# Gating a spatial MLP: the gate value is evicted to one bf16 tile before it is multiplied with z1

## The chip, the core and the metric

The kernel runs on one core of a Trainium2 chip. The metric is device time in microseconds (us), the median of three executions. Engines are named as in the profile: PE is TensorE (matmuls; PEld are its weight loads), DVE is VectorE, ACT is ScalarE, POOL is GpSimd, SP is the engine that issues most of the DMAs.

## The reference

The block first adds a memory-augmented attention to its input and then a gated MLP. The change concerns the MLP alone, whose computation is this (2048 tokens, D = 1024, F = 3584, Fh = 1792):

```
z  = gelu(layernorm(h) @ w_in)                 # [2048, 3584]
z1 = z[:, :1792]
z2 = layernorm(z[:, 1792:])
g  = w_sp @ z2 + b_sp[:, None]                 # over tokens: [2048, 2048] @ [2048, 1792]
h2 = h + (z1 * g) @ w_out
```

Inputs and output are bf16. `z1 * g` is the product that the change is about.

## The kernel before

**The order of the work.** The program is written by hand as a sequence of calls on five engines. A recorder (`_Recorder`, from L30) notes each call with the tiles that it reads and writes, and works out which semaphores it must wait for: the last writer of what it reads, and the last writer and all readers of what it overwrites (`record`, L87; `dep`, L112). For readers and writers on the same engine it waits as well, TensorE excepted; a wait that an earlier instruction of that engine already implies is dropped. `emit` then issues each engine's calls in the recorded order. Each engine thus has one fixed in-order queue, and all instructions show up in the profile under one line, L210, where the recorder issues them; groups are told apart by the names of the tiles.

**The stages.** Attention comes first (to about 340 us of the profile), then the z2 half of the MLP's first matmul with its layernorm, then the z1 half, which leaves z1 transposed in the tile `z1T` (F on the partitions, tokens along the free axis). The first gating stage (`gate(0)`, L1283) gates the first 1024 tokens and writes the product over `z1T` in bf16. Sixteen output units multiply that by `w_out`. The second gating stage (`gate(1)`, L1423) does the other 1024 tokens and writes f16 into `z1x`, which is the same memory under a 16-bit float type of another kind. A last stage multiplies it by `w_out` and writes the output.

**A gating stage.** The product `w_sp @ z2` is done as a two by two block product by seven multiplications in place of eight (Strassen's scheme in Winograd's form). The weight blocks b11, b12, b22, b21 and their sums t1 to t4 are f16 tiles; the sums of z2 blocks (`ss`) are made by VectorE. There are seven groups `g` of 128 columns of F per half. In each, seven products (`prod`, eight matmuls of 128x128 by 128x512 each) go to PSUM banks in the order t2, t1, p1 of a later group (b11), t3, p2 of the next group (b21), t4, b22. Groups 4 and 5 of the second stage have one product fewer. Four output blocks leave each group (c11 is that of the next group): half `i` of F by half `t` of the tokens. Each is made by

- `stt` (L1091): VectorE's scalar_tensor_tensor, one PSUM bank times the scale `inv`, plus a tile. It takes a bank's value down to SBUF and releases the bank, or the accumulation into it, to TensorE.
- `out` (L1094): VectorE's tensor_tensor, the value times a 128x512 part of `z1T`, into `z1T` or `z1x`.

Values and intermediate sums lie in 2 KB fp32 tiles: `u2`, `u3`, `s1b1`, `s1b2`, `s1` (`TMP`, L396; in the profile `tmp_u`, `tmp_s1b`, `tmp_s`). `s1` is p1 scaled, copied from PSUM by ScalarE (`copy1`). POOL adds the bias rows `brow` to it and gets `s1b1` and `s1b2`, which two of the values start from. One group on VectorE runs: `stt` into u2; sums for `ss`; further jobs handed in by the caller (`each`: in the second stage sums of w_out blocks, `ob_sum`, L1376, and in group 6 sums of gated blocks, `y_sum`, L1392); `stt` twice into u3 and `out`; a sum; `c11` of the next group; `stt` into s1b1 and `out`; `stt` into u2 and `out`. TensorE's t4 must wait until the first `stt` of t3 has read bank `bb`, and t3 until `stt` has read t2's value in the same bank.

POOL's add into `s1b1` for the next group overwrites the tile that `out` reads; its add into `s1b2` overwrites one that only `stt` reads.

**Behind the second stage** the last group's sums (`y_sum` on POOL, for one column block) and `o_adds` (L1444, POOL) come before the first output blocks.

Of the kernel before, what the change touches and what calls it, by code (L numbers as in the profile page):

```python
# [5 lines left out]
BF16 = mybir.dt.bfloat16  # L6
# [10 lines left out]
L = 512  # L17
# [241 lines left out]
def bass_sequential_preLN__memory_aug_infini_attn__mixer_gmlp__prompt_kernel(  # L259
# [19 lines left out]
    K = 1024  # L279
# [4 lines left out]
    def tens(name, shape, dt, off):  # L284
        sz = int(np.prod(shape[1:])) * mybir.dt.size(dt)
        assert off % 32 == 0 and off + sz <= ARENA, (name, off, sz)
        t = nc.alloc_sbuf_tensor_at(name, list(shape), dt, offset=abase + off)
        R.space[t[:].tensor.name] = ("sbuf", off)
        return t

    class Bump:
# [4 lines left out]
        def __call__(self, name, shape, dt):  # L296
# [73 lines left out]
          for k, o in ROLES + (("t1", 118), ("t2", 190), ("t3", 22), ("t4", 38))}  # L370
# [24 lines left out]
    BSQ = tens("bsq", [128, 2], F32, 896)  # L395
    TMP = {k: tens("tmp_" + k, [128, L], F32, (4 + 2 * i) * K)  # L396
           for i, k in enumerate(("s1", "s1b1", "s1b2", "u2", "u3"))}
    SJ = [tens("sj%d" % i, [128, T], BF16, (4 + 4 * i) * K) for i in range(2)]
    BROW = [tens("brow%d" % i, [128, L], BF16, (205 + i) * K) for i in range(2)]
    WO0 = [tens("w_out0%d" % i, [128, 7, 512], BF16, o * K) for i, o in enumerate((54, 198))]  # L400
# [10 lines left out]
    def bank(b):  # L411
        return PS[:, b, :]
# [7 lines left out]
    def next_bank():  # L420
        b = rot["banks"][rot["n"] % len(rot["banks"])]
        rot["n"] += 1
        return b
# [333 lines left out]
    vb = [next_bank() for _ in range(2)]  # L757
# [175 lines left out]
    def sp_norm_load(r):  # L933
        sp.dma_start(SJ[r % 2][:], B_w_sp[r * 128:(r + 1) * 128, :])

    def sp_norm(r):
        act.activation(SJ[r % 2][:], SJ[r % 2][:], ACTF.Square, accum_out=SQ[:, r:r + 1])

# [128 lines left out]
    def a_blk(i, j, g):  # L1067
        f = 896 * i + 128 * g
        return Z2H[:, 8 * j:8 * j + 8, f:f + 128]

    def s_sum(k, g):
        if k == 1:
            dve.tensor_tensor(SS[:, 0], a_blk(1, 0, g), a_blk(1, 1, g), ALU.add)
        elif k == 2:
            dve.tensor_tensor(SS[:, 1], SS[:, 0], a_blk(0, 0, g), ALU.subtract)
        elif k == 3:
            dve.tensor_tensor(SS[:, 2], a_blk(0, 0, g), a_blk(1, 0, g), ALU.subtract)
        else:
            dve.tensor_tensor(SS[:, 3], a_blk(0, 1, g), SS[:, 1], ALU.subtract)

    def prod(b, a, w, first):
        for i in range(8):
            pe.matmul(bank(b), a[:, i, :], BH[w][:, i, :], start=(first and i == 0), stop=(i == 7),
                      skip_group_check=True)

    def gate(pr, seam=lambda: None, mid=lambda: None, each=lambda g, k: None):
        inv, zo = (INV[0], Z1T) if pr == 0 else (INVY, Z1X)
        t1, t2 = slice(1024 * pr, 1024 * pr + 512), slice(1024 * pr + 512, 1024 * pr + 1024)
        s1, s1b1, s1b2, u2, u3 = (TMP[k][:] for k in ("s1", "s1b1", "s1b2", "u2", "u3"))

        def stt(o, b, add):  # L1091
            dve.scalar_tensor_tensor(o, bank(b), inv[:], add, ALU.mult, ALU.add)

        def out(v, g, i, t):  # L1094
            dve.tensor_tensor(zo[:, g + 7 * i, t], v, Z1T[:, g + 7 * i, t], ALU.mult)

        def ss(k, g):
            if g < 7:
                s_sum(k, g)

        def p1(g):
            prod(g % 3, a_blk(0, 0, g), "b11", True)

        def copy1(g):
            act.activation(s1, bank(g % 3), ACTF.Copy, scale=inv[:])

        def p2(g):
            prod(g % 3, a_blk(0, 1, g), "b21", False)

        def c11(g):  # L1110
            stt(u3, g % 3, BROW[0][:])
            out(u3, g, 0, t1)

        p1(0)
        copy1(0)
        pool.tensor_tensor(s1b2, s1, BROW[1][:], ALU.add)
        pool.tensor_tensor(s1b1, s1, BROW[0][:], ALU.add)
        p1(1)
        if not pr:
            p1(2)  # L1120
        seam()
        p2(0)
        c11(0)
        for g in range(7):
            bb, bc = 3 + g % 2, 5 + g % 2
            prod(bb, SS[:, 1], "t2", True)
            prod(bc, SS[:, 0], "t1", True)
            stt(u2, bb, s1b2)
            if g == 0:
                mid()  # L1130
            ss(4, g)
            if g:
                ss(1, g + 1)
                ss(2, g + 1)
            if 1 - pr <= g <= 3:
                p1(g + 2)
            each(g, 0)
            prod(bb, SS[:, 2], "t3", False)
            if g < 5:
                copy1(g + 1)  # L1140
                p2(g + 1)
            elif g == 5:
                p1(6)
                copy1(6)
            else:
                p2(6)
            each(g, 1)
            stt(u3, bb, s1b2)
            stt(u3, bc, u3)
            out(u3, g, 1, t2)  # L1150
            if not g:
                ss(1, 1)
                ss(2, 1)
            if g < 6:
                pool.tensor_tensor(s1b2, s1, BROW[1][:], ALU.add)
            ss(3, g + 1)
            if g != 5:
                c11(min(g + 1, 6))
            prod(bb, a_blk(1, 1, g), "t4", False)
            each(g, 2)  # L1160
            stt(s1b1, bb, s1b1)
            out(s1b1, g, 1, t1)
            if g < 6:
                pool.tensor_tensor(s1b1, s1, BROW[0][:], ALU.add)
            prod(bc, SS[:, 3], "b22", False)
            stt(u2, bc, u2)
            out(u2, g, 0, t2)
            each(g, 3)

    fins = {}  # L1170
# [97 lines left out]
    def seam():  # L1268
        sp_half("b21")
        for k in range(1, 4):  # L1270
            s_sum(k, 0)

    def mid():
        for r in range(4):
            sp_sum("t4", r)

    def z1_norm(g, k):
        for h in range(k and 2):
            r, o = 2 * g + (k > 2), 1024 + 512 * h
            if k != 2:  # L1280
                act.activation(bank(7), Z1T[:, r, o:o + 512], ACTF.Square, accum_out=SQY[:, 2 * r + h:2 * r + h + 1])

    gate(0, seam, mid, z1_norm)  # L1283
    pool.tensor_copy(TW[:], TOT[:])
    fin_load(units[0], act)
# [135 lines left out]

    sp.dma_start(Z1T[:, :, 0:512], wout[:, :, 512:D])
    gate(1, each=each1)  # L1423

    def o_prod(b, a, w, first, lo=0, hi=512, cs=range(7)):
# [42 lines left out]
    for g in range(4):  # L1468
        bb, bc = 3 + g % 2, 5 + g % 2
# [63 lines left out]
```

## Time and profile before

| | |
|---|---|
| median of three executions | 758.6 us (758.08 to 759.28) |
| profiled execution | 757.02 us, span 755.3 us |
| TensorE busy | 748.4 us (99%), granted clock 9 of 9 tenths in every slice |
| VectorE busy | 573.4 us (76%) |
| ScalarE, POOL busy | 421.4 us (56%), 294.0 us (39%) |
| first gating stage | about 489 to 574 us |
| second gating stage | about 624 to 710 us |
| in its group 2 (657 to 669 us) | VectorE 11.76 of 12.00 us busy, POOL 2.31, ScalarE 0.69 |

How to read it: a line of the groups gives engine, operation, output tile <- input tiles with partitions x elements and type, the count, then busy time and the mean ns of one, then the engine's idle time before them and what ended it. A timeline line is start, duration (or, for several in a row, their common stretch), engine, operation, tiles and count; in brackets the idle time before it and what ended it. The chain that ended last is followed back from the last instruction: at each step to what released it, or to the instruction before it on its engine. Its lines give start, length and owner. Buffer numbers are left out of tile names, so `tmp_u` is u2 or u3, and `tmp_s1b` is s1b1 or s1b2.

### The profile page before, as it was taken

The page shows a single profiled execution, that of the slowest core. Times are in us where ns is not written, and L with a number is a line of the kernel's source. Part 1 is how long each engine was busy: PE and PEld are TensorE (multiplying, and loading weights), DVE is VectorE, ACT ScalarE, POOL GpSimd, SP SyncE. Part 2 cuts the span into 40 slices and gives each one's busy share as a digit, 9 for nine tenths or more (in the row PEclk, how much of TensorE's full clock was granted, in tenths as well). Part 3 has the DMA queues.
Part 4 walks back from the last instruction along what each step waited for, and adds up shares of the span by engine and source line. Part 5 has one row for each costly group of instructions (what it writes and reads, how often), then busy time and mean ns, then how long its engine had stood idle before and what let it go on. Part 6 is the DMA issues. An engine that isn't in the chain of part 4 may idle for free.

```text
span 755.3 us, 13486 instructions
## 1 busy us (share of the span) xinstructions
PE 748.4 (99%) x5470; PEld 357.9 (47%) x5470; DVE 573.4 (76%) x1013; ACT 421.4 (56%) x519; POOL 294.0 (39%) x450
## 2 busy tenths in 40 slices
PE   8999999999999999999999999999999999999998
PEld 4445455555554445555554444444444444443444
DVE  5585589768974576768896796998895575999876
ACT  6777877787777767226994879723330525300000
POOL 2564456555654333010049988522120001122342
PEclk9999999999999999999999999999999999999999
DMA  9654556454424331678640026320029950001111
GB/s 304 173 160 91 85 78 139 94 79 92 113 58 96 115 72 43 178 195 254 195 141 0 1 56 126 68 86 1 0 41 171 234 196 15 0 1 55 64 49 56
DMA packets 136783, 75.09 MB, mean 99 GB/s; under 512 B 98064, under 2 KB 126480, under 8 KB 136720
## 3 DMA queue, kind: packets, MB, share of 16 engines
q1 hardware_dynamic: 129184, 67.14, 36.9%
q10 hardware_dynamic: 7536, 7.08, 3.2%
q8 instruction: 43, 0.70, 0.4%
q14 instruction: 20, 0.16, 0.1%
HBM read 42.74 MB, written 8.39 MB: 68 GB/s over the span
## 4 chain that ended last, share of the span: by engine, by line
PE 88%; DVE 10%; DMA 1%; issue 1%; POOL 0%; ACT 0%; ACTq 0%; DVEq 0%; POOLq 0%
PE ps L210 88%; DVE z1x L210 3%; DVE tmp_u L210 3%; DVE ss L210 2%; DMA wv<-in_A_wv_dram 1%; DVE tmp_s1b L210 1%; DVE z2h L210 0%; POOL ot L210 0%; DVE sy L210 0%; POOL sy L210 0%; ACT L210 0%; DVE ot L210 0%; DVE fin L210 0%; ACTq L210 0%; DVEq L220 0%
## 5 line engine op out<-in xcount | busy, mean ns | idle before, releaser
L210 ACT ACTIVATE e<-ps 128x2048 bf16<-128x2048 f32 (+1 forms) x96 | 152.7, 1590 | 41.7 <-PE ps L210 41.5
L210 POOL TENSOR_SCALAR_AFFINE_SELECT e<-e 128x512 bf16<-128x512 bf16 x128 | 90.6, 721 | 131.4 <-ACT e L210 131.4
L210 PE MATMUL ps<-win,hnT 128*128 128x448 bf16 x512 | 98.4, 353 | 0.0
L210 POOL TENSOR_TENSOR tmp_s1b<-tmp_s,brow 128x512 f32<-128x512 f32 x28 | 33.6, 1203 | 129.7 <-DVE tmp_u L210 57.4
L210 PEld LDWEIGHTS ps<-win,hnT 128*128 128x128 bf16 x512 | 49.6, 98 | 46.3 <-issue 0.2
L210 PE MATMUL ps<-xnT,wk 128*128 128x512 bf16 x256 | 60.8, 381 | 0.0
L210 PE MATMUL ps<-xnT,wq 128*128 128x512 bf16 x256 | 60.5, 379 | 0.0
L210 PE MATMUL ps<-wv,xnT 128*128 128x512 bf16 x256 | 59.8, 380 | 0.4 <-DVE xnT L210 0.3
L210 DVE TENSOR_TENSOR zt<-ps,zt 128x512 f32<-128x512 f32 x70 | 48.2, 689 | 15.7 <-PE ps L210 12.1
L210 PE MATMUL ps<-wo,oT 128*128 128x512 bf16 x256 | 58.0, 380 | 0.0
L210 ACT ACTIVATE z<-ps 128x448 bf16<-128x448 f32 x60 | 30.6, 548 | 35.0 <-PE ps L210 35.0
L210 PE MATMUL ps<-w_out,z1T 128*128 128x512 bf16 x224 | 48.6, 379 | 0.0
L210 DVE BATCH_NORM_STATS2 zst<-z 128x6 f32<-128x448 bf16 x64 | 38.0, 612 | 10.9 <-ACT z L210 10.9
L210 PEld LDWEIGHTS ps<-v,e 128*128 128x128 bf16 x1280 | 38.8, 96 | 14.0 <-issue 6.5
L210 DVE RECIPROCAL rd<-ps 128x16 f32<-128x16 f32 x32 | 8.0, 250 | 47.1 <-PE ps L210 46.9
L210 ACT ACTIVATE tmp_s<-ps,invy 128x512 f32<-128x512 f32 x7 | 4.8, 687 | 68.0 <-POOL tmp_s1b L210 37.8
L210 PE MATMUL ps<-v,e 128*128 128x33 bf16 x1280 | 42.2, 178 | 0.0
L210 POOL TENSOR_TENSOR sz<-wzh 128x512 f16<-128x512 f16 x28 | 34.5, 1231 | 8.4 <-PE ps L210 8.4
L210 PEld LDWEIGHTS ps<-wo,oT 128*128 128x128 bf16 x256 | 24.0, 98 | 27.6
L210 PEld LDWEIGHTS ps<-xnT,wk 128*128 128x128 bf16 x256 | 22.6, 98 | 29.9 <-issue 5.0
L210 ACT ACTIVATE z1T<-zt,inv 128x512 bf16<-128x512 f32 x42 | 29.0, 715 | 13.1 <-DVE zt L210 13.1
L210 PEld LDWEIGHTS ps<-wv,xnT 128*128 128x128 bf16 x256 | 23.1, 98 | 27.3 <-DVE xnT L210 0.8
(206 smaller groups left out, 1478.0 us busy)
## 6 DMA issues: line engine op xcount, KB each, us to landing
sj<-in_B_w_sp_dram SPq DMA_DIRECT2D x16, 512.0 KB, 3.6
xch<-in_A_x_dram SPq DMA_DIRECT2D x16, 256.0 KB, 3.4
xr<-in_A_x_dram SPq DMA_DIRECT2D x16, 256.0 KB, 3.9
out_dram<-hch SPq DMA_DIRECT2D x16, 256.0 KB, 2.6
win<-in_B_w_in_dram SPq DMA_DIRECT2D x4, 896.0 KB, 5.3
wz<-in_B_w_in_dram SPq DMA_DIRECT2D x6, 512.0 KB, 7.9
wo<-in_A_wo_dram SPq DMA_DIRECT2D x1, 2048.0 KB, 8.4
fin<-out_dram ACTq DMA_DIRECT2D x16, 128.0 KB, 3.0
```

The source lines that it names most:

```text
L210: ins = getattr(e, op.name)(*op.args, **op.kw)
```

## The change

A new tile `VB`, 128x512 in bf16 (1 KB per partition), lies at offset 61 KB, which no tile in use during the gating stages covers. The second `stt` of each output block, whose result is the gate value, writes into it in place of the fp32 tile; `out` reads it there. The first `stt` of u2 and u3, `s1` and POOL's adds stay in fp32. Both gating stages use the same single tile for all four values. `stt` and `out` are as before.

```diff
+    VB = tens("vb", [128, L], BF16, 61 * K)
...
         def c11(g):
-            stt(u3, g % 3, BROW[0][:])
-            out(u3, g, 0, t1)
+            stt(VB[:], g % 3, BROW[0][:])
+            out(VB[:], g, 0, t1)
...
             stt(u3, bb, s1b2)
-            stt(u3, bc, u3)
-            out(u3, g, 1, t2)
+            stt(VB[:], bc, u3)
+            out(VB[:], g, 1, t2)
...
             prod(bb, a_blk(1, 1, g), "t4", False)
             each(g, 2)
-            stt(s1b1, bb, s1b1)
-            out(s1b1, g, 1, t1)
+            stt(VB[:], bb, s1b1)
+            out(VB[:], g, 1, t1)
             if g < 6:
                 pool.tensor_tensor(s1b1, s1, BROW[0][:], ALU.add)
             prod(bc, SS[:, 3], "b22", False)
-            stt(u2, bc, u2)
-            out(u2, g, 0, t2)
+            stt(VB[:], bc, u2)
+            out(VB[:], g, 0, t2)
```

VectorE's instructions are the same in number and order. In the changed program's list the evictions for s1b1 and u2 gain a wait for VectorE's own preceding product, and the first eviction of u2 in the following group loses one.

## The prediction

> **What bounds the kernel now.** I read the page's busy line first, then the chain that ended last in order of time, then TensorE's timeline over both gating stages, then the groups by shape, then the whole timeline of one gating group.
>
> ```profile
> PE 748.4 (99%) x5470; PEld 357.9 (47%) x5470; DVE 573.4 (76%) x1013; ACT 421.4 (56%) x519; POOL 294.0 (39%) x450
> ```
>
> TensorE is never long idle, so no change on VectorE can win more than TensorE's gaps. Where they are, the chain says:
>
> ```profile
> 8.85 625.99 PE ps L210 x4892
> ...
> 634.87 0.76 DVE tmp_u L210
> ...
> 712.02 0.70 DVE z1x L210
> ...
> 716.12 36.09 PE ps L210 x175
> ```
>
> Up to 634.8 us and after 716 us the chain is TensorE alone. Between, which is the second gating stage, it runs through VectorE without a break, ending in POOL's short adds (712.8 to 715.2). There VectorE is late and TensorE is stopped now and then. Busy time hides this, as a matmul's modelled end reaches into the next one; starts show it. In TensorE's timeline eight matmuls normally start in 1.727 us (216 ns each):
>
> ```profile
> 689.54 1.89 PE L210 MATMUL ps<-t1h,ss 128*128 128x512 f16 x8
> 692.08 1.90 PE L210 MATMUL ps<-t3h,ss 128*128 128x512 f16 x8 [0.65 <-DVE tmp_u L210]
> ...
> 713.87 1.89 PE L210 MATMUL ps<-z1x,sy 128*128 128x512 f16 x8
> 716.12 1.69 PE L210 MATMUL ps<-z1x,sy 128*128 128x512 f16 x7 [0.36 <-DVE ot L210]
> ```
>
> 689.54 to 692.08 is 2.54 us, so 0.81 lost; 713.87 to 716.12 is 2.25, so 0.52 lost. All blocks of the two stages read this way give, in the second: before t4 of group 1, 0.64; t3 and t4 of group 4, 0.34 and 0.32; t3 and t4 of group 5, 0.81 and 0.06; t3 of group 6, 0.11; and 0.08 for the blocks behind the stops, which start 0.013 us apart more: 2.36 us. In the first stage t3 of groups 4 and 5 lose 0.10 each, with their tails 0.23. Behind the second, 0.52. Sum 3.11 us: the ceiling.
>
> [...] Both kinds are in the trace:
>
> ```profile
> L210 DVE TENSOR_TENSOR z1T<-tmp_u,z1T 128x512 bf16<-128x512 f32 x21 | 17.9, 852 | 0.7
> ...
> L210 DVE TENSOR_TENSOR z1x<-tmp_s1b,z1T 128x512 f16<-128x512 f32 x7 | 4.8, 692 | 0.2
> ...
> L210 DVE SCALAR_TENSOR_TENSOR fin<-ps,invo,fin 128x512 bf16<-128x512 f32 x4 | 3.0, 749 | 2.0 <-PE ps L210 2.0
> ...
> L210 DVE TENSOR_TENSOR z1x<-z1x 128x512 f16<-128x512 f16 x2 | 0.8, 418 | 0.0
> ```
>
> So a 16-bit product of 512 takes 418 ns against 692, and an eviction that writes bf16 takes 749, the same as the 748 of one that writes fp32: narrowing is free, the product gains. [...]
>
> ```profile
> 661.74 0.96 DVE L210 TENSOR_TENSOR z1x<-tmp_u,z1T 128x512 f16<-128x512 f32 x1
> 662.62 0.68 DVE L210 TENSOR_TENSOR ss<-z2h 128x1024 f16<-128x1024 f16 x1
> ...
> 664.00 0.69 DVE L210 TENSOR_TENSOR z1x<-tmp_u,z1T 128x512 f16<-128x512 f32 x1
> 664.61 0.75 DVE L210 SCALAR_TENSOR_TENSOR tmp_s1b<-ps,invy,tmp_s1b 128x512 f32<-128x512 f32 x1
> 665.38 0.69 DVE L210 TENSOR_TENSOR z1x<-tmp_s1b,z1T 128x512 f16<-128x512 f32 x1
> 666.00 0.74 DVE L210 SCALAR_TENSOR_TENSOR tmp_u<-ps,invy,tmp_u 128x512 f32<-128x512 f32 x1
> 666.15 1.16 POOL L210 TENSOR_TENSOR tmp_s1b<-tmp_s,brow 128x512 f32<-128x512 f32 x1 [4.01 <-DVE z1x L210]
> ...
> 666.77 1.09 DVE L210 TENSOR_TENSOR z1x<-tmp_u,z1T 128x512 f16<-128x512 f32 x1
> 667.89 0.75 DVE L210 SCALAR_TENSOR_TENSOR tmp_u<-ps,invy,tmp_s1b 128x512 f32<-128x512 f32 x1
> ```
>
> Products clear of POOL take 0.69; the one at 666.77, half under POOL's add, takes 1.09. Evictions, with one input in PSUM, are not slowed. [...] Without a wait the next one starts 0.61 us after a product of 0.69 (664.00 to 664.61), with one it starts 0.02 after its end (667.86 to 667.89): a wait costs 0.10. [...]
>
> **The change part by part.**
>
> *The product.* Per group four products hold VectorE, from their start to that of the next instruction, for 0.61 (c11), 0.62 (s1b1), 1.12 (u2), 0.88 (u3): 3.23 us. At 418 ns they are slots of 0.35 without a wait behind, 0.44 with one.
>
> *The waits.* One tile `vb` takes all four values, so each eviction into it must wait until the product before has read it. On VectorE's own order that is a wait on itself. In the changed program's instruction list the evictions for s1b1 and u2, right behind a product, newly carry it (0.44 slots); the first eviction of the next group loses the one it had (u2's slot goes to 0.35); u3's product is followed by a sum (0.35). Nothing but VectorE's own queue stands behind these waits. `vb` lies where the last z1 stage had an input of TensorE, which TensorE has long read when the first gating product it waits for anyway is done: nothing.
>
> *POOL's add into s1b1* waited for the product; now the eviction alone reads `tmp_s1b1`, so the add starts some 0.7 us sooner and lies over s1b1's product in place of u2's. It is not on the path (its sum is next read some 10 us later); its cost is the contention. Lower bound: none, a 0.44 slot. Upper: the trace has a 16-bit sum that takes 0.68 alone and 1.65 wholly under POOL, 41% of the rate; the fp32 product at 666.77 had 0.54 us under POOL and did 0.14 us of work there, 26%. At 41% the 0.42 product takes about 1.02, at 26 to 30% 1.2. I take 1.02, a slot of 1.04. u2's product is then free. POOL's other add starts with the eviction before u3's product and outlives it by 0.39; at the same rate u3's product takes 0.65, a slot of 0.58 (0.35 to 0.60).
>
> *Sum per group:* 0.44 + 1.04 + 0.35 + 0.58 = 2.41, so 0.82 saved (0.6 to 1.65). Over groups 1 to 3 of the second stage VectorE now needs 12.12, 11.86 and 11.86 us (starts of the first u2 eviction at 643.92, 656.04, 667.89, 679.75) where TensorE needs seven blocks, 12.09. In groups 4 and 5 there is one block fewer, 10.36, against VectorE's 11.52 and 10.56: hence the stops. With 0.82 less, VectorE catches up in groups 1 to 3, and group 4 asks for 10.70 against 10.36: 0.34 late, under the slack. That slack is one block, 1.73, less 0.17 for the last matmul's end, 0.77 for the eviction and about 0.08 to TensorE: 0.7. So the stops of both stages go, with perhaps 0.1 left in group 5: 2.36 + 0.23 - 0.1 = 2.5.
>
> *The tail.* In group 6 POOL adds nothing, so its products take 0.42; four of them behind the last t3 bring the last product's end forward by about 1.15 us, and with it POOL's three sums and its add, for which TensorE lost 0.52 at 716.12. What is late next is VectorE's eviction of the first output block: it needs TensorE's product that ends near 714.04, then 0.75 for it and 0.75 for the next one, and TensorE can go on at 715.68 in place of 715.60. So 0.44 is won.
>
> *Everything else* (DMAs, ScalarE, matmuls) issues the same instructions; what VectorE saves beyond this becomes its own idle time. Total 2.5 + 0.4 = 2.9 to 3.0. The profiled execution took 757.02 us with a span of 755.3, so 754.0 and 752.3 are expected; the median, 758.6, lies 1.6 above that execution and the same 3.0 comes off it: 755.6.
>
> **The rivals.** *Part of it.* The contention is at its upper end (1.2) and group 5 still stops TensorE, or the stops of t3 and t4 in groups 4 and 5 (1.6 us) halve only. For it: the 0.7 slack is nearly used there. Against: even the upper end saves 0.6 a group. 756.2 to 757.4.
>
> *The product stays at full length*: mixed types (bf16 by bf16 into f16 in the second stage), or writing over its own input in the first. Against: the profile has 16-bit sums from bf16 into f16 at 680 ns for 1024. Then VectorE has only the new waits, about 0.1 a group net: 758.2 to 759.2.
>
> *Slower: POOL locks s1b1's product out.* POOL's add, now side by side with the product, could hold it until it is done and be stretched as well, as when beside the 16-bit sums (two adds in 2.96 us, against 1.155 alone). The product's slot would be 1.6 + 0.44, u3's 0.8 + 0.44 - together 3.3, where 2.44 is the point at which VectorE needs more than now (3.23 - 0.44 - 0.35). It would lose 0.83 a group, 5.8 us over the seven groups of the second stage, where VectorE already sets the pace: about 764. Against: the 16-bit sum wholly under two adds got through in 1.65 while they ran.
>
> *More.* The median's extra 1.6 us over the profiled execution could lie in these same stops: down to 754.0.
>
> **How the numbers follow.** Forecast (755.0 to 756.3) 0.70; part 0.14; unchanged 0.07; slower 0.05; more 0.04. 0.2%, about what a measurement of this kernel can tell from no change, is 1.5 us. Faster: 0.70 + 0.11 + 0.04 = 0.85; same 0.03 + 0.07 = 0.10; slower 0.05. The range takes forecast and part, 0.84: 754.6 to 757.4.
>
> **What would show it.** Products near 0.42 us and s1b1's between 0.42 and 1.2; VectorE's busy time 12 to 24 us lower; POOL's s1b1 add right behind the eviction; no t3 or t4 block over 1.8 us after the one before; a chain that is TensorE nearly throughout. Products of 0.69, or gaps that stay while VectorE idles between, would refute it.

## The result, and the profile after

The changed kernel takes 755.35 us (755.01 to 755.98, four runs) against 758.94 for the kernel before (758.08 to 759.71, four runs): a ratio of 0.9954, 95% interval 0.9937 to 0.9971. A later measurement gave 755.65 (five runs) against 758.45 (seventeen), 0.9962 (0.9949 to 0.9974). The changed kernel is faster by about 3 us.

The profiled execution took 755.45 us with a span of 753.7, only 1.6 us shorter than before's 755.3. The other 1.4 us are not in the gating: in that execution the first gating stage began at 490.76 us, before's at 489.34. Over all profiles below, of kernels that are the same up to there, it began between 489.34 and 493.28. In after's profile TensorE waits 1.0 us, just before 412.06, for one of POOL's sums of the z1 stage; in before's the only trace of that wait is 0.4 us of a weight load. That is a part of it; the rest is not traced here. This scatter belongs to no version, so I compare traces over the stretch from the first gating product to the end of the span, called the tail stretch below. It is 265.9 us before (from 489.34 to 755.29) and 262.9 after (from 490.76 to 753.67); here and below it is taken from the traces before rounding. These are the two lines its starts come from, each out of TensorE's timeline, first before and then after:

```profile
489.34 4.91 PE L210 MATMUL ps<-b11h,z2h 128*128 128x512 f16 x22
```

```profile
490.76 3.62 PE L210 MATMUL ps<-b11h,z2h 128*128 128x512 f16 x16
```

The busy line of the page after, VectorE 16.3 us lower:

```profile
PE 748.3 (99%) x5470; PEld 359.1 (48%) x5470; DVE 557.1 (74%) x1013; ACT 421.6 (56%) x519; POOL 296.3 (39%) x450
```

The chain that ended last, after: from 412 us to the last output VectorE is no longer in it.

```profile
412.06 338.53 PE ps L210 x1578
750.62 0.62 DVE fin L210
```

TensorE's timeline after, at the places where before showed 2.54 and 2.25 us between starts. 689.47 to 691.20 is 1.73, one normal block; the fifteen matmuls from 712.78 take 3.24 us, 216 ns each. What is left of the stops is one of 0.09 us, at 684.28, 1.81 after the block before:

```profile
682.47 1.89 PE L210 MATMUL ps<-b21h,z2h 128*128 128x512 f16 x8
684.28 1.90 PE L210 MATMUL ps<-t4h,z2h 128*128 128x512 f16 x8
...
689.47 1.89 PE L210 MATMUL ps<-t1h,ss 128*128 128x512 f16 x8
691.20 1.89 PE L210 MATMUL ps<-t3h,ss 128*128 128x512 f16 x8
...
712.78 3.40 PE L210 MATMUL ps<-z1x,sy 128*128 128x512 f16 x15
716.02 1.67 PE L210 MATMUL ps<-w_out0h,z1x 128*128 128x512 f16 x7
```

The groups by shape, after. The products have a mean of 482 ns where most had 869; the evictions are as long as ever:

```profile
L210 DVE TENSOR_TENSOR z1x<-vb,z1T 128x512 f16<-128x512 bf16 x28 | 13.5, 482 | 1.0
...
L210 DVE SCALAR_TENSOR_TENSOR vb<-ps,invy,tmp_u 128x512 bf16<-128x512 f32 x14 | 10.5, 751 | 1.0 <-PE ps L210 0.5
```

And the same group as was shown of before, in the whole timeline:

```profile
661.05 1.16 POOL L210 TENSOR_TENSOR tmp_s1b<-tmp_s,brow 128x512 f32<-128x512 f32 x1 [6.59 <-DVE tmp_u L210]
...
661.79 0.70 DVE L210 TENSOR_TENSOR z1x<-vb,z1T 128x512 f16<-128x512 bf16 x1
...
663.79 0.42 DVE L210 TENSOR_TENSOR z1x<-vb,z1T 128x512 f16<-128x512 bf16 x1
664.25 0.75 DVE L210 SCALAR_TENSOR_TENSOR vb<-ps,invy,tmp_s1b 128x512 bf16<-128x512 f32 x1
665.03 0.42 DVE L210 TENSOR_TENSOR z1x<-vb,z1T 128x512 f16<-128x512 bf16 x1
665.08 1.40 POOL L210 TENSOR_TENSOR tmp_s1b<-tmp_s,brow 128x512 f32<-128x512 f32 x1 [2.87 <-DVE vb L210]
...
666.28 0.48 DVE L210 TENSOR_TENSOR z1x<-vb,z1T 128x512 f16<-128x512 bf16 x1
...
667.13 0.75 DVE L210 SCALAR_TENSOR_TENSOR tmp_u<-ps,invy,tmp_s1b 128x512 f32<-128x512 f32 x1 [0.37 <-PE ps L210]
```

The last line shows the roles reversed: VectorE now waits for TensorE (0.37 us) ahead of the eviction that in before it reached too late. The line at 665.03 is the surprise: this product lies under POOL's add and still takes 0.42; it is the add that takes 1.40.

### The profile page after: what moved, and what is told of

Its sections match the earlier page's. It is cut to its first block, busy times and chain, and to the rows that moved or that the text cites. A ratio compares the mean times of both kernels' runs of the same rounds, so it can differ in the third digit from the quotient of the medians.

```text
span 753.7 us, 13510 instructions
## 1 busy us (share of the span) xinstructions
PE 748.3 (99%) x5470; PEld 359.1 (48%) x5470; DVE 557.1 (74%) x1013; ACT 421.6 (56%) x519; POOL 296.3 (39%) x450
## 4 chain that ended last, share of the span: by engine, by line
PE 90%; DMA 3%; ACT 3%; DVE 2%; POOL 2%; issue 0%; ACTq 0%; DVEq 0%
PE ps L210 90%; DMA sj<-in_B_w_sp_dram 2%; ACT sj L210 2%; POOL zrs L210 1%; DMA wv<-in_A_wv_dram 1%; POOL sz L210 1%; DVE zst L210 1%; ACT z L210 1%; DVE wzh L210 1%; DVE ht L210 0%; DVE zmv L210 0%; ACT L210 0%; DVE fin L210 0%; ACTq L210 0%; DVE top L210 0%
## 5 line engine op out<-in xcount | busy, mean ns | idle before, releaser
L210 POOL TENSOR_TENSOR tmp_s1b<-tmp_s,brow 128x512 f32<-128x512 f32 x28 | 36.4, 1301 | 121.6 <-DVE tmp_u L210 63.0
```

Source lines behind the costliest of these rows:

```text
L210: ins = getattr(e, op.name)(*op.args, **op.kw)
```

## The experiments

My theory: TensorE's stops, nearly all in and behind the second stage, are the whole gain, and they go because VectorE spends less time per group. The rivals: VectorE time counts everywhere alike; the separate tile, not the short product, is what helps; a part of the gain is only the new place of POOL's add. The kernel before was timed beside each of them; ratios are to those runs.

### One stage alone

Two kernels that use `VB` in one stage and the fp32 tiles in the other:

```diff
+        def vb(o):
+            return VB[:] if pr == 1 else o      # or pr == 0
-            stt(VB[:], bc, u3)
-            out(VB[:], g, 1, t2)
+            stt(vb(u3), bc, u3)
+            out(vb(u3), g, 1, t2)
```

and so for the other three values.

> The bf16 value in the second gating stage alone, fp32 in the first. Theory (the gain is TensorE's stops, which lie nearly all in the second stage and behind it): 2.7 to 3.0 us under the kernel before, that is near 755.8, with the 0.10 us stops before t3 of groups 4 and 5 of the first stage still there. Rival (every microsecond that VectorE saves counts, in either stage alike): half of the gain, near 757.1.

> The bf16 value in the first gating stage alone. Theory: only the first stage's 0.2 us of stops go, so 0.0 to 0.4 us under the kernel before, near 758.5; the stops of the second stage stay at about 2.4 us and 0.5 behind it. Rival (saved VectorE time counts alike in both): half of the gain, near 757.1.

Measured: second stage alone 755.92 us against 758.30, ratio 0.9967 (0.9955 to 0.9980); first stage alone 758.16, ratio 0.9997 (0.9988 to 1.0005). Tail stretches: 263.1 and 265.7 us. So the second stage brings 2.8 us (2.4 by the medians) and the first 0.2 of the 3.0; saved VectorE time does not count alike. The stops stay where the theory puts them. TensorE's timeline of the kernel with the first stage alone, group 5 of the second stage:

```profile
691.19 1.89 PE L210 MATMUL ps<-t1h,ss 128*128 128x512 f16 x8
693.73 1.90 PE L210 MATMUL ps<-t3h,ss 128*128 128x512 f16 x8 [0.65 <-DVE tmp_u L210]
```

2.54 us again, to the hundredth. And of the kernel with the second stage alone, group 4 of the first stage, 1.83 us between the starts, 0.10 more than a block:

```profile
546.30 1.89 PE L210 MATMUL ps<-t1h,ss 128*128 128x512 f16 x8
548.13 1.90 PE L210 MATMUL ps<-t3h,ss 128*128 128x512 f16 x8
```

### The tile without the short product

```diff
-            dve.tensor_tensor(zo[:, g + 7 * i, t], v, Z1T[:, g + 7 * i, t], ALU.mult)
+            dve.scalar_tensor_tensor(zo[:, g + 7 * i, t], v, 1.0, Z1T[:, g + 7 * i, t], ALU.mult, ALU.mult)
```

> The changed kernel, tile, waits and types kept, but the product done by a scalar_tensor_tensor (value times 1.0 times z1), [...]690 to 760 ns in place of 420. Theory (the length of the product is what counts): the stops come back, 758.5 to 760. Rival (the separate tile counts, since it frees the fp32 tiles and lets POOL's add into s1b1 start before the product): stays at 755.4 to 756.0.

Measured: 757.23 us (21 runs), ratio 0.9986 (0.9980 to 0.9993); tail stretch 264.8. Products at full length:

```profile
L210 DVE SCALAR_TENSOR_TENSOR z1x<-vb,z1T 128x512 f16<-128x512 bf16 x28 | 21.0, 751 | 1.0
```

Neither forecast holds. My theory said that all stops come back, the rival that none does; 1.2 of the 3.0 us of gain are left. The stop before t3 of group 5 is 0.59 in place of 0.81, those of the first stage are gone. The timeline of this kernel's second stage explains a part: the product for u2 takes 0.74 and not 1.09, since POOL's add now falls on s1b1's product, which is not lengthened.

```profile
666.34 0.69 DVE L210 SCALAR_TENSOR_TENSOR z1x<-vb,z1T 128x512 f16<-128x512 bf16 x1
666.38 1.66 POOL L210 TENSOR_TENSOR tmp_s1b<-tmp_s,brow 128x512 f32<-128x512 f32 x1 [3.40 <-DVE vb L210]
```

### The short product without the tile

Each eviction writes bf16 into the front half of its own fp32 tile:

```diff
-    VB = tens("vb", [128, L], BF16, 61 * K)
+    VB = {k: tens("vb_" + k, [128, L], BF16, o * K) for k, o in (("s1b1", 6), ("u2", 10), ("u3", 12))}
```

with `stt` and `out` taking the tile of their value.

> bf16 values without the shared tile: each eviction writes bf16 into the front half of the fp32 tile that the kernel before used (u3, s1b1, u2), so the added waits of VectorE on itself go and POOL's add into s1b1 again waits for the product. Theory: products stay at 420 ns, TensorE is the bound, the time is that of the changed kernel, 755.2 to 755.8. Rival 1 (the single tile's waits, some 0.2 us a group, are on the path): about 1 us faster, 754.3. Rival 2 (POOL's earlier add is a part of the gain): 756.5 or more.

Measured: 755.41 us (seven runs), ratio 0.9967 (0.9955 to 0.9979); tail stretch 262.9, that of the changed kernel. Both rivals fall: the single tile's waits are hidden, and POOL's earlier add is not needed once the product is short. Here the add is back behind s1b1's product and u2's product pays for it, at 0.82 or 0.66 us as the case may be; the path does not notice:

```profile
656.15 1.16 POOL L210 TENSOR_TENSOR tmp_s1b<-tmp_s,brow 128x512 f32<-128x512 f32 x1 [3.21 <-DVE z1x L210]
656.77 0.82 DVE L210 TENSOR_TENSOR z1x<-vb_u,z1T 128x512 f16<-128x512 bf16 x1
```

### POOL's earlier add alone

To see what of the 1.2 us came from the order of POOL's add: the kernel before, all in fp32, with

```diff
-            stt(s1b1, bb, s1b1)
-            out(s1b1, g, 1, t1)
+            stt(u3, bb, s1b1)
+            out(u3, g, 1, t1)
```

> The kernel before, all in fp32, with one edit: the eviction for s1b1 writes u3 (free then) and its product reads it there, so that POOL's add into s1b1 starts beside that product, as in the changed kernel. If the full-length experiment's 1.1 us came from this order alone: s1b1's product 0.69 with POOL's add stretched to about 1.66, u2's product near 0.74 in place of 1.09, some 0.9 to 1.1 us under the kernel before (757.4), and from the first gating matmul to the end 264.8 to 265.0 us in place of 265.9. If most of it came from the wait that the next group's first eviction loses: less than half of that, 758.2, 265.4 or more.

Measured: 757.86 us (13 runs) against 758.45, ratio 0.9991 (0.9983 to 0.9999); tail stretch 265.1, so 0.8 us of the 1.2, a little less than expected. s1b1's product takes 0.69 with an add of 1.66 beside it, as expected; u2's takes 0.87, not 0.74. In the full-length experiment two more things differ: the next group's first eviction has no wait on u2's product, and its products are another operation. The traces point to the first for the remaining 0.3 to 0.4 us. From s1b1's product to the next group's first eviction it is 2.18 us there (654.70 to 656.88) and 2.30 here (654.33 to 656.63), and that eviction starts 0.07 us before the end of u2's product there and 0.04 after it here. A run that changes this wait alone was not made, so it is not shown.

### More and less VectorE time

Three kernels move VectorE's time per group and leave the product's type alone. The changed kernel with an unneeded eviction:

```diff
             stt(VB[:], bb, s1b1)
+            stt(u3, bb, BROW[0][:])
             out(VB[:], g, 1, t1)
```

> The changed kernel with one unneeded eviction per group (128x512, 0.75 us, into u3, which is free then) between the eviction for s1b1 and its product. VectorE's four product slots, about 2.1 us a group in the changed kernel, and this one come to about 2.9 to 3.0, near the 3.23 of before. Theory (margin of VectorE against TensorE in groups 4 to 6 decides): most stops are back, 757 to 758.5. Rival (VectorE is off the path once the products are short): 755.4 to 755.9.

Measured: 756.91 us (20 runs) against 758.50, ratio 0.9977 (0.9970 to 0.9984); tail stretch 264.2. About 1.3 of the 3.0 us are lost again: t3 of group 5 waits 0.53 us once more. VectorE is not off the path for good; it has a margin, and 0.7 us per group for the eviction with 0.5 more for the product, which now starts under POOL's add, uses it up. That the stops come back by less than half was not what I expected.

Both kernels without the fourth z2 sum in groups 1 to 6:

```diff
-            ss(4, g)
+            if not g:
+                ss(4, g)
```

> The changed kernel without the fourth z2 sum (0.6 us of VectorE) in groups 1 to 6 of both stages: those products take a stale sum, so that part of the computation is left out. Theory (TensorE is the bound, 0.09 us of stops are left): 755.2 to 755.5, no change. Rival (VectorE's queue still sets the pace of the second stage): 0.6 x 6 = 3.6 us off, near 752.

> The kernel before without the same sum in groups 1 to 6 of both stages (that part of the computation is left out), its products in fp32. Theory (any VectorE time taken out of a group removes the stops): 0.6 a group removes most of them, 2 to 2.8 us under the kernel before, near 756.3. Rival (it is the 16-bit operand as such, not VectorE's time, that helps TensorE): as before, 758.6.

Measured, in the changed kernel: 756.07 us (five runs, 754.83 to 757.05), ratio to before 0.9967 (0.9953 to 0.9981), no faster than the changed kernel and above the 755.2 to 755.5 expected; but the tail stretch is 262.9, the same to a tenth. So with the short products TensorE is the bound, and more VectorE time saved brings nothing. In the kernel before: 757.11 us (19 runs), ratio 0.9982 (0.9975 to 0.9989); tail stretch 264.5. Stops go without any 16-bit operand, so the rival falls, but 1.4 us is less than the 2 to 2.8 expected. Group 5's stop hardly moved (2.52 us between starts, 0.79 lost):

```profile
689.88 1.89 PE L210 MATMUL ps<-t1h,ss 128*128 128x512 f16 x8
692.40 1.90 PE L210 MATMUL ps<-t3h,ss 128*128 128x512 f16 x8 [0.63 <-DVE tmp_u L210]
```

So the place of the saved time counts as well as its amount. On VectorE all four products of a group lie between two evictions that TensorE waits for: that of t3's product, which t4 needs, and that of t2's product, which t3 of the next group needs. The omitted sum lies in the other part, from t2's eviction to t3's. In before's timeline the two evictions around the products of groups 4 and 5 are

```profile
683.55 0.74 DVE L210 SCALAR_TENSOR_TENSOR tmp_u<-ps,invy,tmp_s1b 128x512 f32<-128x512 f32 x1
...
691.27 0.75 DVE L210 SCALAR_TENSOR_TENSOR tmp_u<-ps,invy,tmp_s1b 128x512 f32<-128x512 f32 x1
```

From the end of the first to the end of the second VectorE takes 7.73 us. TensorE has four blocks in that time (t4, b22, t2, t1), 6.91 us. The difference is 0.82, and the stop before t3 of group 5 is 0.81. The same stretch accounts for that stop in the other kernels: 7.73 us without the sum (stop 0.79), 7.64 with POOL's earlier add alone (0.72), 7.51 with full-length products in the tile (0.59), 7.45 with the extra eviction (0.53), and 6.44 in the changed kernel, less than the four blocks, and no stop.

### Who waits, POOL or VectorE

```diff
             stt(VB[:], bb, s1b1)
+            dve.scalar_tensor_tensor(u3[:, 0:128], PS[:, bb, 0:128], inv[:], BROW[0][:, 0:128], ALU.mult, ALU.add)
             out(VB[:], g, 1, t1)
```

> The changed kernel with a short unneeded eviction (128x128, about 0.34 us) at the same place, so that s1b1's product starts about 0.35 us after POOL's add and no longer 0.04 before it. Reading 1 [...]: the product takes about 1.0 to 1.1 us, ending 0.28 after the add, and the add is back at 1.16 us from 1.39. Reading 2 [...]: the product takes 0.75 to 0.85 and the add stays stretched, near 1.4. Time 756 to 757.5 by either.

Measured: 756.32 us (17 runs), ratio 0.9973 (0.9964 to 0.9981), tail stretch 264.0.

```profile
653.62 0.34 DVE L210 SCALAR_TENSOR_TENSOR tmp_u<-ps,invy,brow 128x128 f32<-128x128 f32 x1
653.78 1.16 POOL L210 TENSOR_TENSOR tmp_s1b<-tmp_s,brow 128x512 f32<-128x512 f32 x1 [2.87 <-DVE vb L210]
653.88 1.34 DVE L210 TENSOR_TENSOR z1x<-vb,z1T 128x512 f16<-128x512 bf16 x1
```

The product starts only 0.10 us after the add, less than meant, and so is longer than my 1.0 to 1.1; but it ends at 655.22, 0.28 after the add (654.94), and the add is back at 1.16. These are the lengths of reading 1: the add, which starts first, keeps its own, and the product is held until 0.28 us after the add's end. The 0.28 recurs wherever a 16-bit product starts under an add: 662.49 against 662.21 in the changed kernel, 657.59 against 657.31 in the one with own tiles. For the fp32 products of before it is 0.55: 667.86 against 667.31.

In the kernel with the whole extra eviction the product starts 0.49 us after the add and again ends 0.28 after it. The end of the product hangs on the add, so VectorE's stretch around the products is 7.45 us in both kernels, and they lose nearly the same (1.1 and 1.3 us of the tail stretch), though one unneeded eviction is less than half as long as the other.

### The changed kernel again

> The changed kernel unaltered, beside the kernel before on the same chip, for a tighter ratio and a second profile: 3.0 us (2.7 to 3.4) under the kernel before; from the first gating matmul to the end 262.9 us as in the first profile, one stop of 0.09 us left in the two gating stages, while the start of the gating may differ by a microsecond or two.

Measured: 755.65 against 758.45 us, as given above, 2.8 us less; tail stretch 262.9, with one stop of 0.09 us.

## Why the prediction was right

The forecast was 755.6 us, range 754.6 to 757.4; measured 755.35 and 755.65. By its steps:

*The ceiling.* The sum of TensorE's stops, 3.11 us, was the right quantity: the tail stretch fell by 3.0. The one-stage kernels split it as the sum did: 2.36 + 0.52, less the 0.09 that stayed, for the second stage and behind it against 2.8 measured, and 0.23 for the first against 0.2. In all twelve traces, with stops from 0.1 to 3.1 us, the tail stretch less the stops, summed over both gating stages and the blocks just behind the second, is 262.8 us. So the stops are the whole difference between these kernels from the first gating product on.

*The product and the eviction.* 418 ns was forecast for a product clear of POOL, 0.42 measured; 749 for a narrowing eviction, 751 measured. VectorE's busy time fell by 16.3 us, inside 12 to 24.

*The waits and the buffer.* The added waits on itself cost VectorE their 0.1 us (0.46 from 663.79 to 664.25, where 0.44 was taken; with own tiles, without the wait, 0.34 from 655.65 to 655.99) and nothing on the path: own tiles gave the same 262.9.

*POOL's add.* This term was mis-sized. The prediction took a shared rate and gave s1b1's product 1.02 us, u2's 0.42 and u3's 0.65; they took 0.42, 0.48 and 0.70. The traces show no shared rate in such a pair. The one that starts second ends a set time behind the first: the short product 0.28 us behind the add, the add 1.01 behind the product, and s1b1's product starts 0.04 or 0.05 us before the add. The trace of before already had the like. The prediction's 41% came from a 16-bit sum beside POOL's adds:

```profile
492.51 1.40 POOL L210 TENSOR_TENSOR tmp_s1b<-tmp_s,brow 128x512 f32<-128x512 f32 x1 [8.19 <-ACT tmp_s L210]
492.82 1.65 DVE L210 TENSOR_TENSOR ss<-z2h 128x1024 f16<-128x1024 f16 x1
```

The add ends at 493.91 and the sum 0.55 us later, as the fp32 products do. Two more sums of that size in before, at 494.50 and 696.98, start 0.62 and 0.47 us behind the start of an add, where this one starts 0.31 behind, and end 0.55 after it as well. So the end of the add set the sum's length; 41% is no rate. The slots from each product's start come to 0.63 + 0.46 + 0.46, and about 0.48 for u2's if VectorE's wait of 0.37 is taken off: 2.03 in place of 2.41, 1.2 saved a group and not 0.82. The error did not touch the time, but by little: in the stretch around the products 7.73 less 0.82 is 6.91, just TensorE's four blocks. That the product comes first, by 0.04 us, was not foreseen, and this was luck. In the late-product kernel the end of the product follows the add as it would if the add came first, and 1.1 us of the gain were lost; by that estimate the time would have been near 756.5, in the stated range but above what was forecast.

*What is left.* 0.1 us was expected in group 5, from lateness carried over. 0.09 is there, but in group 4 and with VectorE waiting 0.38 us for TensorE first, as the z2 sum at 680.94 must wait until t1 has read its tile. The size is right; the cause given was not.

*The tail.* 0.44 was forecast with 0.08 left over; all of the 0.52 went.

*The rivals.* "Part of it" did not happen. "The product stays at full length" fell on the 482 ns. "Slower" had the product held until the add is done. The late product was held so, at 1.34 us; in the changed kernel it starts 0.04 us ahead and takes 0.42. Even where it was held, the add was not stretched (1.16), and the kernel was still 1.9 us faster than before in the tail stretch. "More", that the median's extra 1.6 us over the profiled execution lie in these stops, found no support. The kernel with the first stage alone has the second stage of before; its profiled execution took 758.68 us, 1.66 more than before's, with the same stops in and behind that stage. The tail stretch of both profiles of the changed kernel is the same to a tenth. What scatters between these executions lies ahead of the gating.

Where my reasoning was too simple is the total per group. It forecast the outcome, but my expectations for the full-length product and for the omitted sum each missed by about a microsecond, in opposite directions: more gain was left with the first, and less came with the second. The two evictions that TensorE waits for split the group, and once TensorE has stopped for one of them, the part of VectorE's queue up to the next had to fit TensorE's blocks by itself (7.73 us against 6.91 before t3 of group 5).

## What to carry to other kernels

Where TensorE is 99% busy, add up the gaps between the starts of its blocks and take that sum as the most that a faster VectorE can bring; here it was 3.11 us and 3.0 came, though VectorE saved 16. Cut VectorE's queue at the instructions that TensorE waits for and compare each part with TensorE's work in the same time: the stop before t3 fell only when the part ahead of it, 7.73 us against 6.91, became shorter. When a VectorE product and a POOL add, each of two SBUF tensors, overlap, look at which of them starts first, by hundredths of a microsecond: here the product took 0.42 us when it started 0.04 ahead of the add, and 1.34 when it started 0.10 behind.

## What the runs showed of the hardware

A VectorE product with two SBUF inputs and a POOL add with two SBUF inputs ended as if they ran one after the other, the second some 0.14 us sooner than its own length behind the first (0.28 for 0.42, 0.55 for 0.69, 1.01 for 1.155; the 0.14 is my estimate from these). Started 0.04 or 0.05 us ahead of the add, the product kept its 0.42 (full length: 0.69), and the add, ending 1.01 after it, went from 1.16 to 1.40 (beside a full-length product: 1.66). Started 0.10 us (late product) to 1.20 us (u2's product in the changed kernel) behind the start of an add, the product ended 0.28 us after the add (full length: 0.55) whatever its start, and took up to 1.34, and it did not lengthen the add: 1.16 beside the late product. So in these runs the price of such a pair depended on the order of two starts and fell on one of the two alone. Evictions, with one input in PSUM, took 0.75 under the add as elsewhere.
